# Reordering a pipelined turn and the closing sequence of a fused RWKV-6 and Mixture-of-Depths kernel

## The chip, the cores and the metric

The kernel runs on one core of a Trainium2 chip. The metric is device time in microseconds of one execution. A core has a matrix engine (TensorE, PE in the profile), a vector engine (VectorE, DVE), an activation engine (ScalarE, ACT), a general one (GpSimd, POOL) and a queue for transfers (SyncE, SP). Each engine works through its own list of instructions in order and waits for the others through semaphores. PEld is TensorE's loading of weights.

## The reference

Two blocks follow one another. The first is a recurrent attention (RWKV-6): for each of 4 batches and 8 heads, over 768 steps with head size 48,

```python
cur = einsum('bhd,bhe->bhde', u[None] * kt, vt)
y[:, :, t] = einsum('bhd,bhde->bhe', rt, state + cur)
state = wt[:, :, :, None] * state + einsum('bhd,bhe->bhde', kt, vt)
```

Its output, heads side by side, is x of 4 x 768 x 384. The second (Mixture of Depths) takes in each batch the 128 rows with the highest score and adds a gated MLP to them alone:

```python
scores = einsum('bsd,d->bs', x, w_gate)
top_idx = argpartition(-scores[b], capacity)[:capacity]
ye = maximum(xe @ w1, 0) @ w2          # 384 -> 1024 -> 384
out[b, top_idx] = x[b, top_idx] + sigmoid(scores[b, top_idx])[:, None] * ye
```

## The kernel before

The time axis is cut in chunks of 128 steps, six to a batch, 24 in all. Within a chunk the recurrence becomes matrix products: `scans` multiplies up the decays from both ends (two VectorE scans, from right and from left, read from the transposed w in PSUM), `scaled` makes K and R from the transposed k and r, `scores` multiplies them (ps_s), `masked` keeps the strictly earlier steps (sc), `outputs_t` multiplies sc with v and R with the state carried over (ps_yt), and `carry_products` and `carry` make the next state (kv, then mid and state). `back` transposes K back into kt, which only `carry_products` reads. The diagonal term, r times k times u summed over a head, is made apart: `own_products` (two GpSimd products), `own_values` (eight ScalarE sums, each an activation and a read of the accumulator, lines L293, and then a GpSimd product with v, L297). `rows_out` transposes the result to rows (ps_y), copies it out on ScalarE, adds the diagonal term on GpSimd and stores it. `row_products` and `row_sums` make the row's score. `range_check` sums over w on ScalarE (junk), for a check at the end.

The order is written by hand: `turn(i)` issues the steps of up to five neighbouring chunks, from chunk i + 2 (decays) to chunk i - 2 (comparing scores). Every engine takes its instructions in the order in which they are issued there. `loads(i + 5)` issues the inputs of the turns to come on SP's queue, in buffers that rotate over four or five chunks; in the first turns one weight tile is loaded per turn as well.

For the choice of rows, `compared_t` transposes a chunk's scores over all partitions (ps_e, in the bank of psK) and copies them to `every` on ScalarE; `compared` compares the chunk with earlier ones and with itself (`ahead`, with counts in `lost`). When a batch is complete, `mixture(b)` becomes a generator that goes on piece by piece: ranks by 21 small matmuls with ones (ps_r) and three small VectorE operations; `pick`, a comparison of the ranks with slot numbers; ps_i, the row numbers; an indirect gather of 128 rows (xe); their transposition; and last the gate (scr_x on GpSimd, a sum and an exponential on ScalarE, two small VectorE operations). Each yield carries a place, "half" or "end", and `mix(place=...)` goes on only where the place fits.

`forward` is the MLP of one batch, a generator too, of 8 pieces of ps_h (three 128x128 matmuls, each two instructions) and 8 of ps_f; then ye and an indirect scatter. `fed_in_turn` puts up to three pieces into a turn, except for batch B - 2, whose MLP is kept for the end, where it stands between the steps of the last batch. The last batch's ps_f is made in two halves of columns, each with its own ye and scatter.

Pools of PSUM with one buffer each: psW (w transposed), psS (scores and outputs), psY (rows), psK (kv, ps_e, ranks, row numbers), psM (MLP); psT (transposed k, r, K) has two. An instruction that takes a buffer waits until the one before it in that buffer has been read.

After the last turn the code lists the pieces by hand, then `checked()` reduces the range check and loads its result in a register of every engine (L264), which decides whether a general version has to run. For these inputs it doesn't.

## Time and profile before

| | us |
|---|---|
| median of 3 runs | 223.97 |
| lowest, highest | 223.69, 226.28 |
| the profiled execution, its own time | 226.24 |
| its span, first to last instruction | 224.4 |
| TensorE busy in the span | 197.57 (88%) |
| VectorE | 164.20 (73%) |
| ScalarE | 143.46 (64%) |
| GpSimd | 135.01 (60%) |

All rows of the profile come from one execution. Its own time is 1.84 us longer than the span from the first instruction to the last. A line such as L236 is the kernel's line, or that of a helper (L223 makes all transpositions, L281 makes K and R). The mean granted clock of TensorE over the span is 0.99. "idle" is the time in which an engine stood still before an instruction, and the arrow names what ended it. Durations of neighbouring instructions on an engine overlap a little, so the pitch from start to start is used where instructions are added up.

### The profile page before, as it was taken

What the parts mean: (1) busy time and instruction counts of PE and PEld (TensorE: products, weight loads), DVE (VectorE), ACT (ScalarE), POOL (GpSimd) and SP (SyncE); (2) the same over time, 40 slices, a digit from 0 to 9 for tenths busy, and PEclk for the clock granted to TensorE, in tenths of its full rate; (3) what the DMA queues carried; (4) which work ended last, traced back from release to release, by engine and by line L of the source; (5) the groups of instructions that cost most, each with busy time, mean ns of one, the idle gap of its engine ahead of it and who ended that gap; (6) DMA issues with size and microseconds to landing.
All of it is one profiled execution on the core that took longest, in us unless ns stands there. A gap on an engine that the chain in (4) does not pass through costs nothing.

```text
span 224.4 us, 6400 instructions
## 1 busy us (share of the span) xinstructions
PE 197.6 (88%) x2306; PEld 162.9 (73%) x2306; DVE 164.2 (73%) x370; ACT 143.5 (64%) x697; POOL 135.0 (60%) x158
## 2 busy tenths in 40 slices
PE   2699998898798699998999999989999989896990
PEld 1489877776676578977877788879787768764990
DVE  6979978899897977779987798698869863632010
ACT  6256977987777577777867686895766784512110
POOL 2335988776785498477558579864854965413011
PEclk9999999999999999999999999999999999998898
DMA  7999999998999788775996597479611201102000
GB/s 122 183 166 178 187 180 233 189 215 222 222 220 186 167 202 173 108 144 99 137 151 129 86 174 158 114 141 162 133 46 36 73 35 38 72 0 75 1 22 25
DMA packets 105687, 29.20 MB, mean 130 GB/s; under 512 B 100512, under 2 KB 104896, under 8 KB 105648
## 3 DMA queue, kind: packets, MB, share of 16 engines
q1 hardware_dynamic: 105104, 27.14, 67.3%
q0 software_dynamic: 544, 1.57, 2.3%
q8 instruction: 20, 0.33, 0.6%
q14 instruction: 19, 0.16, 0.2%
HBM read 23.20 MB, written 5.51 MB: 128 GB/s over the span
## 4 chain that ended last, share of the span: by engine, by line
PE 39%; ACT 28%; DVE 21%; issue 8%; POOL 1%; DMA 1%; POOLq 0%; DVEq 0%
ACT rk L293 13%; PE ps_t L223 8%; DVE right_buf L236 7%; PE ps_s L306 6%; PE ps_f L570 6%; PE ps_h L547 5%; ACT junk L270 4%; PE ps_yt L335 4%; DVE left L248 3%; ACT x L365 3%; PE ps_kv L396 3%; ACT kt L320 3%; DVE ahead L449 3%; PE ps_w L223 3%; PE ps_y L223 2%
## 5 line engine op out<-in xcount | busy, mean ns | idle before, releaser
L293 ACT ACTIVATE rk<-rk 128x48 f32<-128x48 f32 x192 | 43.8, 240 | 0.0
L367 POOL TENSOR_TENSOR x<-x,vo 128x384 f32<-128x384 f32 x23 | 23.0, 1001 | 30.4 <-ACT x L365 27.7
L293 ACT ACTIVATION_READ_ACCUMULATOR rk<-rk 128x1 f32 x192 | 38.0, 198 | 0.0
L315 DVE TENSOR_TENSOR sc<-ps_s,before_f 128x512 f32<-128x512 f32 x48 | 30.8, 682 | 4.1 <-PE ps_s L306 3.1
L248 DVE TENSOR_TENSOR_SCAN left<-ps_w,from_left 128x511 f32<-128x511 f32 x24 | 30.7, 1280 | 0.9
L236 DVE TENSOR_TENSOR_SCAN right_buf<-ps_w,from_right 128x511 f32<-128x511 f32 x24 | 29.2, 1218 | 0.7 <-PE ps_w L223 0.5
L306 PE MATMUL ps_s<-R,K 48*128 48x128 f32 x384 | 28.8, 291 | 0.1
L335 PE MATMUL ps_yt<-sc,v_buf 128*64 128x128 f32 x384 | 27.1, 284 | 1.6 <-PE ps_w L223 1.2
L547 PE MATMUL ps_h<-xeT,w 128*128 128x128 f32 x192 | 26.9, 293 | 1.8 <-DVE x L361 0.7
L286 POOL TENSOR_TENSOR rk<-r_buf,k_buf 128x384 f32<-128x384 f32 x24 | 24.1, 1006 | 7.2 <-DMA r_buf<-in_r_dram 7.2
L306 PEld LDWEIGHTS ps_s<-R,K 48*128 48x128 f32 x384 | 24.1, 193 | 4.3 <-issue 3.7
L547 PEld LDWEIGHTS ps_h<-xeT,w 128*128 128x128 f32 x192 | 24.4, 203 | 3.3 <-ACT xeT L514 1.2
L335 PEld LDWEIGHTS ps_yt<-sc,v_buf 128*64 128x64 f32 x384 | 21.4, 140 | 6.1 <-issue 2.8
L287 POOL TENSOR_TENSOR rk<-rk,u_bc 128x384 f32<-128x384 f32 x24 | 24.1, 1004 | 2.5 <-DMA u_bc<-in_u_dram 0.7
L372 POOL TENSOR_TENSOR scr<-x,wg_bc 128x384 f32<-128x384 f32 x23 | 23.0, 1000 | 1.8
L570 PE MATMUL ps_f<-w,hid 128*128 128x384 f32 (+1 forms) x80 | 23.8, 432 | 0.0
L320 ACT COPY kt<-ps_t 128x512 f32<-128x512 f32 x24 | 13.8, 575 | 14.4 <-PE ps_t L223 14.4
L281 DVE TENSOR_TENSOR R<-ps_t,left 128x512 f32<-128x512 f32 x24 | 16.5, 688 | 8.8 <-ACT x L365 2.7
L297 POOL TENSOR_TENSOR vo<-v_buf,own 128x384 f32<-128x384 f32 x24 | 19.9, 830 | 3.4 <-ACT rk L293 3.4
L223 PE MATMUL ps_w<-ident,w_buf 128*128 128x128 f32 x96 | 15.8, 291 | 4.8 <-DVE from_right L208 4.1
L348 ACT COPY yt<-ps_yt 128x512 f32<-128x512 f32 x24 | 14.1, 587 | 9.2 <-PE ps_yt L343 7.7
L449 DVE SCALAR_TENSOR_TENSOR ahead<-ps_e,score,after_f 128x128 bf16<-128x128 f32 x24 | 8.4, 350 | 15.7 <-ACT every L436 15.7
(98 smaller groups left out, 377.2 us busy)
## 6 DMA issues: line engine op xcount, KB each, us to landing
w_buf<-in_w_dram SPq DMA_DIRECT2D x24, 192.0 KB, 4.6
k_buf<-in_k_dram SPq DMA_DIRECT2D x24, 192.0 KB, 4.7
r_buf<-in_r_dram SPq DMA_DIRECT2D x24, 192.0 KB, 5.2
v_buf<-in_v_dram SPq DMA_DIRECT2D x24, 192.0 KB, 4.2
out_dram<-x SPq DMA_DIRECT2D x24, 192.0 KB, 2.5
w<-in_moe_w_dram SPq DMA_DIRECT2D x3, 512.0 KB, 5.9
w<-in_moe_w_dram SPq DMA_DIRECT2D x4, 384.0 KB, 6.2
u_bc<-in_u_dram SPq DMA_DIRECT2D x1, 192.0 KB, 4.6
```

The source lines that it names most:

```text
L223: nc.tensor.transpose(ps[:, j, :], src(j), ident)
L236: nc.vector.tensor_tensor_scan(out=flat[:, W - 2::-1], data0=wt[:, W - 1:0:-1], data1=from_right.rearrange("p j t -> p (j t)")[:, W - 2::- ...
L248: nc.vector.tensor_tensor_scan(out=left.rearrange("p j t -> p (j t)")[:, 1:W], data0=wt[:, 0:W - 1], data1=start.rearrange("p j t -> p (j ...
L286: nc.gpsimd.tensor_mul(rk, r_bufs[n % NBUF][:, :, 0:D], k_bufs[n % NBUF][:, :, 0:D])
L287: nc.gpsimd.tensor_mul(rk, rk, u_bc)
L293: nc.scalar.activation(out=rk[:, h, :], in_=rk[:, h, :], func=AF.Copy, accum_out=o[:, h:h + 1])
L306: nc.tensor.matmul(ps[:, q, j, :], t["K"][rows, j, :], t["R"][rows, j, :], start=True, stop=True,)
L315: nc.vector.tensor_mul(t["sc"][:, q], ps[:, q], _heads(before_f, HP))
L335: nc.tensor.matmul(ps[half(c), j % 2, j // 2, :], vt[:, 2 * j + q, :], t["sc"][:, q, j, :], start=(j < 2), stop=(old is None), skip_group_ ...
L367: nc.gpsimd.tensor_add(x, x, vo.rearrange("p h d -> p (h d)"))
L547: nc.tensor.matmul(ps[:, q, :], w1[:, dc, (f0 + q) * L:(f0 + q + 1) * L], xeT[:, dc, :], start=(dc == 0), stop=(dc == NDC - 1),)
L570: nc.tensor.matmul(ps, hid[:, fc, :], w2[:, fc, cols], start=(fc == 0), stop=(fc == NFC - 1))
```

## The change

The steps of a turn are issued in another order, some are split, and the closing sequence is another. What each engine's list shows:

- In the turn: `own_values` (ScalarE) right after `scores`; the second GpSimd product of `own_products` becomes `own_weights`, later in the turn; the product with v becomes `own_results`, later too; the one-element copy of `scans` becomes `first_left`, after `back`; `range_check` goes ahead of the outputs and `row_sums` ahead of the scans.
- `compared_t` and `compared` become one step, ahead of `masked`. Its ps_e lies in psW instead of psK, and the copy to `every` comes after the comparisons.
- `back` is left out for the last chunk of a batch.
- `mixture`: the rank matmuls use minus one, run with the later chunk outermost, and one more matmul (identity times `lost`) adds the counts; one reduction makes the rank. Ranks and `pick` are made in one piece. `pick` is six operations of 128 columns with a bf16 source.
- `fed_in_turn` gives batch B - 2 at most one piece per call, where it gave none.
- The last batch's ps_f, ye and scatter are no longer halved.
- The last two chunks' rows are added and scored on VectorE, where it was the last one's alone.
- In the end all 16 pieces of the last batch's MLP are issued ahead of `checked()`, and the gate after it, since the transposition of xe is now reached before. On TensorE the matmul of the range check stands behind the last ps_f; on GpSimd and ScalarE the load of the register stands ahead of scr_x and its sum.
- Memsets that are left to the framework's choice of engine fall out in another way at the start; from_right goes from ScalarE to VectorE.

```diff
-    ones = consts.tile([L, L], BF16)
-    nc.vector.memset(ones, 1.0)
+    minus = consts.tile([L, 1], BF16)
+    nc.vector.memset(minus, -1.0)
...
-    slots = consts.tile([L, L], FP32)
+    slots = consts.tile([L, L], BF16)
...
-        nc.scalar.copy(out=left[:, 0, 0:1], in_=start[:, 0, 0:1])
...
+    def first_left(t):
+        start = from_left[t["n"] % len(from_left)]
+        nc.scalar.copy(out=t["left"][:, 0, 0:1], in_=start[:, 0, 0:1])
...
-        nc.gpsimd.tensor_mul(rk, rk, u_bc)
+
+    def own_weights(t):
+        nc.gpsimd.tensor_mul(t["rk"], t["rk"], u_bc)
...
+    def own_results(t):
         t["vo"] = lev.tile([L, H, D], FP32, tag="vo", name="vo", bufs=3)
         nc.gpsimd.tensor_mul(
-            t["vo"], v_bufs[t["n"] % VBUF][:, :, 0:D], o.to_broadcast([L, H, D])
+            t["vo"], v_bufs[t["n"] % VBUF][:, :, 0:D], t.pop("own").to_broadcast([L, H, D])
         )
...
     def back(t):
+        if chunks[t["n"]][1] == NCH - 1:
+            return
...
-        t["e"] = ps = psK.tile([L, L], FP32, tag="kv", name="ps_e")
-        nc.tensor.transpose(ps, score[:, b, ci:ci + 1].to_broadcast([L, L]), ident)
-        if ci < NCH - 1:
-            nc.scalar.copy(out=against[b][0][:, ci * L:(ci + 1) * L], in_=ps)
...
+        ps = psW.tile([L, L], FP32, tag="w", name="ps_e")
+        nc.tensor.transpose(ps, own.to_broadcast([L, L]), ident)
         if ci > 0:
             nc.vector.tensor_scalar(
                 out=ahead[:, ci, 0:lo], in0=every[:, 0:lo], scalar1=own, scalar2=None,
                 op0=ALU.is_ge, op1=ALU.add, accum_out=lost[:, ci, 0:1],
             )
         nc.vector.scalar_tensor_tensor(
-            out=ahead[:, ci, lo:hi], in0=t.pop("e"), scalar=own, in1=after_f,
+            out=ahead[:, ci, lo:hi], in0=ps, scalar=own, in1=after_f,
             op0=ALU.is_ge, op1=ALU.mult, accum_out=lost[:, ci, 1:2],
         )
+        if ci < NCH - 1:
+            nc.scalar.copy(out=every[:, lo:hi], in_=ps)
...
+        for e in range(NCH):
+            for c in range(e + 1):
                 nc.tensor.matmul(
-                    ps[:, c:c + 1], ahead[:, e, c * L:(c + 1) * L], ones[:, 0:1],
-                    start=(e == c), stop=(e == NCH - 1),
-                )
+                    ps[:, c, 0:1], ahead[:, e, c * L:(c + 1) * L], minus,
+                    start=(e == 0), stop=False, skip_group_check=True,
+                )
+            if e == NCH - 2 and ended:
+                yield "half"
+        against.pop(b)
+        nc.tensor.matmul(
+            ps.rearrange("p c k -> p (c k)"), ident, lost.rearrange("p c k -> p (c k)"),
+            start=False, stop=True, skip_group_check=True,
+        )
         rank = mod.tile([L, NCH], FP32, name="rank", bufs=2)
-        nc.vector.tensor_add(rank, lost[:, :, 0], lost[:, :, 1])
-        nc.vector.tensor_add(rank, rank, behind_n)
-        nc.vector.tensor_sub(rank, rank, ps)
-        yield "end"
+        nc.vector.tensor_reduce(out=rank, in_=ps, axis=AX.X, op=ALU.add)
...
-            nc.vector.tensor_tensor(
-                out=pick, in0=_heads(slots, NCH), in1=at.to_broadcast([L, NCH, L]),
-                op=ALU.is_equal,
-            )
+            for c in range(NCH):
+                nc.vector.tensor_scalar(
+                    out=pick[:, c, :], in0=slots, scalar1=at[:, c:c + 1], scalar2=None,
+                    op0=ALU.is_equal,
+                )
...
-        if not (feed or picked) or (feed or picked)[0][0] != B - 2:
-            fed(n, on=False)
+        kept = (feed or picked) and (feed or picked)[0][0] == B - 2
+        fed(min(n, 1) if kept else n, on=False)
...
     def turn(i):
+        soon = i >= N - 1
         step(own_products, i + 1)
         step(scores, i)
+        step(own_values, i)
         step(scaled, i + 1, "K", "right")
         step(carry, i - 1, work.get(i))
+        step(own_weights, i + 1)
+        if i < N:
+            step(compared, i - 2)
         step(masked, i)
         step(back, i)
+        step(first_left, i + 1)
         mix(place="half")
-        if i == N:
-            fed(2)
-        step(rows_out, i - 1, i == N)
-        if i == N:
-            row_scores_soon(work[N - 1], work[N - 1]["x"])
-        else:
-            step(row_products, i - 1)
-        step(own_values, i)
+        step(rows_out, i - 1, soon)
+        step(row_scores_soon if soon else row_products, i - 1)
+        step(own_results, i)
         fed_in_turn(PIECES // 2)
         step(inputs_t, i + 1, "R", r_bufs)
-        step(compared_t, i - 2)
         step(scaled, i + 1, "R", "left")
         step(decays_t, i + 2)
-        step(compared, i - 2)
+        step(range_check, i + 2)
         step(outputs_t, i)
+        if i == N - 1:
+            step(compared, i - 1)
         step(carry_products, i)
         fed_in_turn(PIECES - PIECES // 2)
         step(inputs_t, i + 2, "K", k_bufs)
+        if not soon:
+            step(row_sums, i - 1)
         step(scans, i + 2)
-        step(range_check, i + 2)
-        if i < N:
-            step(row_sums, i - 1)
...
         ended.append(True)
-        fed(2)
-        step(compared_t, N - 1)
+        mix(1000)
+        mixing.append([mixture(B - 1), "half"])
+        mix()
         step(compared, N - 1)
-        mixing.append([mixture(B - 1), "half"])
         fed(2)
         mix()
         fed(1)
         mix()
-        fed(3)
+        fed(NFC - 1)
         mix()
+        fed(1)
         fed(2 * NFC)
         outside = checked()
         mix(1000)
```

## The prediction

> **What bounds the kernel now.** I read the page's busy shares first (TensorE 197.57 us of a span of 224.4, then VectorE 164, ScalarE 143, GpSimd 135), then the chain of waits, then the table of waits, then busy time turn by turn, and last the timeline of the end. No engine fills the span, so the chain says what holds it. One turn of the steady stretch:

> ```profile
> 41.82 1.80 ACT rk L293 x16
> 44.16 1.15 DVE right_buf L236
> 45.93 0.62 ACT junk L270 x2
> 46.57 0.64 ACT junk L270 x2
> 47.78 0.47 ACT kt L320
> 48.25 0.44 ACT x L365 x2
> 48.69 1.80 ACT rk L293 x16
> ```

> The columns are start, length and work. From one rk to the next is 6.87 us, and the chain goes from ScalarE to VectorE and back: VectorE can't start its scans before ScalarE has done rk and `every`, and ScalarE stands at the one-element copy L247 until VectorE's reciprocal. The table of waits (total, times, longest) has both crossings:

> ```profile
> ACT left L247 <- DVE from_left L244: 22.7, 21, 2.6
> ...
> DVE ahead L449 <- ACT every L436: 15.7, 18, 2.5
> ```

> Neither engine is full: the two wait for each other. TensorE by turn (from one chunk's first ps_s to the next; columns are window, length, then busy time and count of PE, weight loads, DVE, ACT, POOL, then clock, DMA share, GB/s):

> ```profile
> 38.53:45.40 6.87, 6.25 (x86) 5.03 (x86) 6.14 (x14) 5.46 (x28) 5.25 (x7) 1.00 1.10 208
> ...
> 65.82:73.65 7.83, 6.87 (x108) 5.50 (x107) 6.23 (x16) 5.56 (x28) 5.47 (x7) 1.00 0.96 229
> 73.65:81.99 8.34, 6.50 (x92) 5.12 (x91) 7.10 (x16) 5.56 (x28) 5.12 (x7) 1.00 0.76 175
> ...
> 114.48:122.93 8.45, 8.45 (x114) 6.68 (x113) 6.49 (x17) 5.77 (x29) 5.47 (x7) 1.00 0.74 124
> ```

> Turns without MLP pieces leave TensorE idle 0.6 to 1.8 us; with three pieces (some 2.1 us) it is full. So the first third has room to lose, the rest little. Last, the end:

> ```profile
> 204.31 0.14 DVE L261 TENSOR_SCALAR wide<-ps_w 1x1 int32<-1x1 f32 x1 [0.28 <-PE ps_w L259]
> ...
> 205.25 1.00 POOL L522 TENSOR_TENSOR scr_x<-xe,wg_bc 128x384 f32<-128x384 f32 x1
> ...
> 207.36 0.16 DVE L531 RECIPROCAL gate<-gate 128x1 f32<-128x1 f32 x1
> ...
> 218.62 0.42 DVE L577 SCALAR_TENSOR_TENSOR ye<-ps_f,gate,xe 128x192 f32<-128x192 f32 x1 [2.12 <-PE ps_f L570]
> 219.87 0.99 POOL L580 DMA_INDIRECT out_dram<-ye,to  x1 [2.13 <-DMA out_dram<-ye,to]
> ```

> The range check (`wide`) and the gate's scr_x are done under the last MLP, long before ye needs the gate.

> **The loop, turns 2 to 22.** own_values goes ahead of the turn's other ScalarE work, L247 moves behind kt, `every` behind `ahead`, the compare ahead of `sc`. The mutual wait goes. What then sets a turn? By the pitches in the timeline, VectorE needs K 0.58, mid 0.26, own compare 0.27, sc 1.19, R 0.60, right 1.26, all 0.19, reciprocal 0.22, left 1.20 = 5.77, and for the compare with earlier chunks 0 to 0.80 by its place in the batch (mean 0.45): 6.2. TensorE: ps_s 1.09, K back 0.60, ps_y 0.49, r 0.49, ps_e 0.12, ps_w 0.58, ps_yt 1.02 + 0.62, kv 0.60, k 0.59 = 6.2. ScalarE: 1.80 + 0.25 + 0.47 + 0.09 + 0.44 + 1.33 + 0.50 + 0.51 = 5.4. GpSimd 5.3. So 6.87 becomes about 6.3, with TensorE and VectorE both nearly full.

> The change adds one wait here: ps_e now takes the single psW bank, so it waits for the left scan, and ps_w behind it waits until `ahead` and `every` have read ps_e. On TensorE, K back, ps_y, r and ps_w queue behind ps_e, and the right scan waits for ps_w. Walking it from ps_e at 0: `ahead` starts 0.35 to 0.8, `every` ends some 0.65 later, at 1.0 to 1.45; TensorE, busy with K, y and r, comes to ps_w at 1.7. Hidden by 0.25 or more; uncovered, the whole handshake would be 1.5 us a turn. L247, late behind kt, ends at 1.6 to 2.0 and R wants it at 1.8: nothing to 0.2.

> Skipping `back` for the last chunk of a batch takes 4 transposes (0.60) from TensorE and one kt (0.47) from ScalarE, four times. Its turn then has 5.0 us of TensorE work and VectorE decides, at 5.5 to 6.3.

> The mixture: two small adds of VectorE (0.2 each) become one reduce (bounds 0.16 and 0.3, from the small reduce of 0.19 at L257), two more copies a batch 0.2, and a matmul with 18 columns (0.1 to 0.3). The pick becomes six 128-column operations with a bf16 source. The trace has none; nearest is L445 at 128x128 (pitch 0.27, with an accumulator read of 0.08 in it): 0.2 each, 1.2 against 0.85; lower bound 0.08 each, as of tiny operations. Ranks and pick move a turn up, so ps_i no longer stands behind a fresh pick: it idled 1.64 in turn 9.

> [...] The old pick (0.93 to 0.96 us, two SBUF sources) never met a GpSimd operation in this trace: GpSimd was idle from 75.06 while it ran at 75.18, and likewise later. The new one falls beside x<-x,vo (1.0 us). [...]

> Turn sums: 2 to 4, 20.15 -> 18.85 (6.25 + 6.3 + 6.3). Turns 5 to 9, 36.59 -> 32.5 (5.7, 6.2, 7.1, 7.0, 6.5: VectorE in 5 and 6, then TensorE waiting once for sc). Turns 10 to 22 lose their TensorE idle of 4.0 us and two `back` (1.2) and get back some 1.0 for extra instructions and one VectorE-bound turn: -4.2. Together -9.6. I take off 1.9, some 0.09 a turn, for hand-overs that an addition of pitches doesn't see: -7.7.

> **The tail.** Before, from the last chunk's ps_s (186.59) to the gather's issue (201.11) is 14.52. After: ps_s 1.09; ps_e and `ahead` to 1.75; sc to 2.94; ps_yt to 4.62; yt and one MLP piece to 5.5; ps_y 6.05; x and score on VectorE to 7.25; two pieces and 15 rank matmuls keep TensorE until 8.05; ps_e, own compare to 8.7; but two pieces stand in front of the last six ranks, to 9.7; lost, reduce 10.35; picks 11.5, ps_i chasing them; gather at about 12.0. Gain 2.5. It lands 3.2 later at 15.2, but seven ps_f pieces (4.7) hold TensorE to 16.2; ps_x then, against 18.45: -2.2.

> Those seven pieces fill the gap in which TensorE went cold:

> ```profile
> 206.13:209.50 3.37, 3.37 (x16) 3.37 (x17) 0.37 (x3) 0.82 (x3) 0.12 (x1) 0.51 0.08 27
> 209.50:213.00 3.50, 3.50 (x33) 3.50 (x33) 0.00 (x0) 0.60 (x1) 0.00 (x0) 0.99 0.00 0
> ```

> Granted clock 0.51, 16 matmuls where 33 fit next. [...] After the change only 0.6 us (xeT) stays idle; ps_h takes 48 x 0.128 = 6.1, not 7.06. [...] ps_f's end comes 3.2 earlier counted from ps_s.

> Then the loss. The new order issues all 16 pieces of the last batch before the range check, and the gate's part after it. The range check's matmul now stands behind the last ps_f, the register load of `wide` (0.515 on GpSimd, 0.464 on ScalarE) behind that, and GpSimd's scr_x and ScalarE's sum behind the load, with ye and the scatter waiting for the gate. From the end of ps_f: ps_w to `wide` and load 0.39 + 0.515, to scr_x 1.05; scr_x to reciprocal's end 2.27 (205.25 to 207.52); 0.62 for a whole ye (its 128x384 row); 0.28 to the scatter: 4.25. Before, the second scatter left 1.29 after ps_f's end, as it waited for the first one's landing. +3.0. One scatter of whole rows for two: its landing is 3.0 against 2.4, +0.3 taken. Tail: -3.2 + 3.0 + 0.3 = +0.1. TensorE's second MLP pieces moved into turn 23 are in this walk.

> Start: memsets change engines; from_right ends near 3.5 on VectorE while ps_w starts at 4.10: nothing, at most 0.4.

> **Sum.** 224.4 - 7.7 + 0.1 = 216.8 of span. The profiled execution took 226.24, 1.84 around the span, and lies at the top of the three runs (223.69, 223.97, 226.28); I take the same -7.6 from the median: 216.4.

> **Rivals.**
> - *The turns shrink, the tail pays* (0.15). The gather is not earlier or the clock still drops: the 3.2 is missing: 219.6. For: two MLP pieces stand ahead of the last ranks. Against: TensorE's work there is counted.
> - *DMA holds the first third* (0.12). The share is 1.10 at 208 GB/s in the turns that also load weights. Turns 2 to 9 keep their length, only 4.2 less 1.0 is won: 220.9. Against: past the start no wait there is for a load, which are issued turns ahead.
> - *The psW handshake* (0.08), on the other side. If ScalarE comes late to `every` (rk in front of it still running), ps_w and the right scan follow. The ScalarE round of x, GpSimd's two products, row sum, rk, `every` adds to 5.6; beyond 6.3 it decides, and at 7.2 the eight early turns gain 0.3 each and the full ones a bubble of as much on TensorE: 21 x 0.3 = 6.3 less 2.4 from `back` and 2.4 from the mixture's move (some 1.9 in turn 9, 0.5 in turn 8), and +0.1: 225.6.
> - *No hand-over losses* (0.10): -9.6, tail -0.5: 213.9.
> - Forecast, 216.4, own range 214.6 to 218.8 (0.55).

> **Numbers.** A measurement of this kernel tells some 2% from no change, so faster is below 219.5: forecast 0.55, no losses 0.10, about half of the tail case 0.07 and a little of DMA 0.02: 0.74. Slower than 228.4 needs the handshake at more than its price: 0.05. The rest 0.21. The range 213.7 to 221.2 leaves out the handshake and the outer edges.

> **What would show it.** Right: L247's successor no longer waits; turns 3 and 4 near 6.3; turn 9 near 6.5; the gather some 12 us after the last ps_s; clock near 1 through the last ps_h; and, on the bad side, over 4 us from the last ps_f to the only scatter. Wrong: waits of ps_w for `every`, or of the right scan for ps_w, in every turn; early turns still at 6.9; the pick stretched to a microsecond.

## The result, and the profile after

| | before | after |
|---|---|---|
| median, us (4 runs each) | 225.12 (223.69 to 226.62) | 215.79 (215.43 to 216.8) |
| ratio, 95% interval | | 0.9592 (0.9505 to 0.9679) |
| the profiled execution | 226.24 | 215.43 |
| its span | 224.4 | 213.6 |
| start, up to ps_s of chunk 2 | 25.25 | 24.27 |
| turns 2 to 22 | 161.34 | 151.70 |
| from the last chunk's ps_s to the end | 37.81 | 37.63 |

The forecast was 216.4. The three parts of the span changed by -0.98, -9.64 and -0.18, in all -10.8, where the forecast had 0, -7.7 and +0.1. The medians differ by 9.3, less than the spans, since the profiled execution lay near the top of its runs before and is the lowest one after. In the medians and ranges from here on all runs count, in the ratios only those within 1.5% of the fastest of the same kernel (with three moves six of ten, with the compare alone three of four).

The chain of waits (start, length, work), one turn of the same stretch that was shown of before:

```profile
36.28 1.09 PE ps_s L313 x16
...
38.94 0.45 PE ps_w L223 x4
39.39 0.19 issue
39.58 1.09 PE ps_yt L344 x16
...
42.45 1.09 PE ps_s L313 x16
```

Before, the chain went from ScalarE to VectorE and back. Here every piece is TensorE's own, and a turn takes 6.17 us where it took 6.87. Over the whole span 80% of the chain lies on TensorE, where it was 39%, with 28% on ScalarE and 21% on VectorE. The table of waits (total, times, longest):

```profile
ACT yt L357 <- PE ps_yt L352: 17.4, 19, 2.0
ACT every L460 <- DVE ahead L455: 12.9, 14, 1.4
...
ACT left L255 <- DVE from_left L244: 1.5, 1, 1.5
```

ScalarE's wait for the reciprocal has gone from 22.7 us to 1.5; VectorE's wait for `every` (15.7) is no longer there. ScalarE waits elsewhere instead, and in the turn shown those waits cost nothing: the chain doesn't pass through it. Busy time by turn (window, length, then busy time and count of PE, weight loads, DVE, ACT, POOL, clock, DMA share, GB/s):

```profile
36.21:42.38 6.17, 5.96 (x87) 5.05 (x86) 6.07 (x14) 5.50 (x30) 5.23 (x7) 1.00 1.01 229
...
68.09:75.30 7.21, 6.36 (x92) 5.17 (x91) 7.00 (x18) 5.02 (x27) 4.73 (x6) 1.00 1.05 201
106.98:115.64 8.66, 8.66 (x115) 6.89 (x115) 7.86 (x20) 5.60 (x30) 5.22 (x6) 1.00 0.72 129
```

In the first, TensorE and VectorE are both nearly full, as the walk through the turn had said. In the second, VectorE is at 7.00 of 7.21: there the pick of the turn before is paid (below). In the third, full of MLP, TensorE fills the turn. The closing sequence, from the timeline:

```profile
204.22 0.15 DVE L264 TENSOR_SCALAR wide<-ps_w 1x1 int32<-1x1 f32 x1 [11.07 <-PE ps_w L262]
205.10 0.99 POOL L536 TENSOR_TENSOR scr_x<-xe,wg_bc 128x384 f32<-128x384 f32 x1 [10.76 <-DVE wide L264]
...
207.39 0.62 DVE L578 SCALAR_TENSOR_TENSOR ye<-ps_f,gate,xe 128x384 f32<-128x384 f32 x1
208.29 1.02 POOL L581 DMA_INDIRECT out_dram<-ye,idx  x1 [2.20 <-DVE ye L578]
```

ps_f ended at 204.06. All four rows stand behind it: VectorE and GpSimd had waited 11 us for the range check's matmul, and the scatter leaves 4.23 after ps_f's end, where the second one of before left 1.29 after it. Busy time in a window over the last ps_h (columns as in the table by turn):

```profile
193.30:196.67 3.37, 3.37 (x30) 3.37 (x31) 0.00 (x0) 0.35 (x1) 1.03 (x1) 1.00 0.15 58
```

30 matmuls at a clock of 1.00, where 16 at 0.51 stood in an equal window before.

### The profile page after: what moved, and what is told of

Read it like the earlier page. It is cut to its first block, busy times and chain, and to the rows that moved or that the text cites. A ratio compares the mean times of both kernels' runs of the same rounds, so it can differ in the third digit from the quotient of the medians.

```text
span 213.6 us, 6385 instructions
## 1 busy us (share of the span) xinstructions
PE 190.9 (89%) x2282; PEld 157.4 (74%) x2282; DVE 166.3 (78%) x388; ACT 140.3 (66%) x688; POOL 131.5 (62%) x155
## 4 chain that ended last, share of the span: by engine, by line
PE 80%; ACT 4%; DVE 3%; issue 3%; DMA 3%; POOL 2%; SPq 2%; POOLq 0%
PE ps_t L223 13%; PE ps_s L313 11%; PE ps_yt L344 11%; PE ps_h L561 11%; PE ps_f L571 10%; PE ps_yt L352 5%; PE ps_kv L406 5%; PE ps_y L223 4%; PE ps_w L223 4%; PE ps_e L449 3%; DMA k_buf<-in_k_dram 3%; ACT rk L298 2%; SPq L132 1%; DVE sc L322 1%; PE ps_r L474 1%
## 5 line engine op out<-in xcount | busy, mean ns | idle before, releaser
L298 ACT ACTIVATION_READ_ACCUMULATOR rk<-rk 128x1 f32 x192 | 36.1, 188 | 0.0
L376 POOL TENSOR_TENSOR x<-x,vo 128x384 f32<-128x384 f32 x22 | 22.1, 1005 | 19.4 <-ACT x L374 19.2
L247 DVE TENSOR_TENSOR_SCAN left<-ps_w,from_left 128x511 f32<-128x511 f32 x24 | 30.7, 1281 | 0.9
L236 DVE TENSOR_TENSOR_SCAN right_buf<-ps_w,from_right 128x511 f32<-128x511 f32 x24 | 29.1, 1211 | 0.9 <-PE ps_w L223 0.8
L344 PE MATMUL ps_yt<-sc,v_buf 128*64 128x128 f32 x384 | 26.3, 278 | 2.4 <-PE ps_w L223 1.7
L561 PE MATMUL ps_h<-xeT,w 128*128 128x128 f32 x192 | 25.4, 280 | 1.1 <-ACT xeT L528 0.8
L344 PEld LDWEIGHTS ps_yt<-sc,v_buf 128*64 128x64 f32 x384 | 20.7, 136 | 6.8 <-PE ps_w L223 3.3
L561 PEld LDWEIGHTS ps_h<-xeT,w 128*128 128x128 f32 x192 | 22.9, 192 | 2.4 <-ACT xeT L528 1.3
L571 PE MATMUL ps_f<-w,hid 128*128 128x384 f32 x64 | 23.8, 499 | 0.3 <-ACT hid L566 0.3
L381 POOL TENSOR_TENSOR scr<-x,wg_bc 128x384 f32<-128x384 f32 x22 | 22.0, 1002 | 1.7
L284 DVE TENSOR_TENSOR K<-ps_t,right_buf 128x512 f32<-128x512 f32 x24 | 16.2, 677 | 6.2 <-PE ps_t L223 6.2
L422 POOL TENSOR_TENSOR state<-mid,all 128x192 f32<-128x192 f32 x16 | 8.1, 507 | 16.9 <-PE ps_s L313 11.5
```

What stands on the lines that cost most here:

```text
L236: nc.vector.tensor_tensor_scan(out=flat[:, W - 2::-1], data0=wt[:, W - 1:0:-1], data1=from_right.rearrange("p j t -> p (j t)")[:, W - 2::- ...
L247: nc.vector.tensor_tensor_scan(out=left.rearrange("p j t -> p (j t)")[:, 1:W], data0=wt[:, 0:W - 1], data1=start.rearrange("p j t -> p (j ...
L284: nc.vector.tensor_mul(out, t.pop(name + "t"), t.pop(by))
L298: nc.scalar.activation(out=rk[:, h, :], in_=rk[:, h, :], func=AF.Copy, accum_out=o[:, h:h + 1])
L344: nc.tensor.matmul(ps[half(c), j % 2, j // 2, :], vt[:, 2 * j + q, :], t["sc"][:, q, j, :], start=(j < 2), stop=(old is None), skip_group_ ...
L561: nc.tensor.matmul(ps[:, q, :], w1[:, dc, (f0 + q) * L:(f0 + q + 1) * L], xeT[:, dc, :], start=(dc == 0), stop=(dc == NDC - 1),)
```

## Experiments: which move makes the loop faster

Turn n is the time from chunk n's first ps_s to the next chunk's. The theory after the result was that of the prediction: the mutual wait of ScalarE and VectorE held the turn, and three moves end it. The rival was that one of them does all. First each move alone in the kernel before. Ratios in this part are to the kernel before.

**The copy of one element behind kt.**

```diff
-        nc.scalar.copy(out=left[:, 0, 0:1], in_=start[:, 0, 0:1])
...
         step(back, i)
+        step(first_left, i + 1)
```

> The kernel before with one edit: the one-element copy L247 leaves the scans and stands behind kt, as in the changed kernel. Ring theory (ScalarE waits for VectorE's reciprocal and VectorE for ScalarE's every; cutting one of the two crossings is enough): early turns fall from 6.87 to about 6.3, ScalarE's wait for the reciprocal (22.7 us) goes, time 3 to 4 us under the kernel before (225.1), near 221.5. Rival (each of the three moves gives its share of the loop's gain): about 1 us less, 224. Rival (the copy is tiny and its wait idle time that costs nothing): no difference.

Measured: 224.28, ratio 0.9946 (0.9917 to 0.9975). The wait at the copy is gone (1.4 us left of 22.7), early turns are 6.49 to 6.56, and VectorE still waits 13.7 us for `every`; turns 2 to 22 are 2.0 shorter. Cutting this crossing is not enough for the 221.5 of the ring theory: the gain is that of its first rival, and the other half of the mutual wait stays. How far such a sum repeats: the filler kernel (below) has the loop of the kernel before, and there turns 2 to 22 took 162.13 for 161.34, the 0.8 coming with a fall of TensorE's clock to 0.50 for 3.4 us in turn 9.

**The sums rk early.**

```diff
         step(scores, i)
+        step(own_values, i)
...
-        step(own_values, i)
+        step(own_results, i)
```

> The kernel before with one edit: the eight ScalarE sums rk are issued right behind ps_s, ahead of kt and x, the GpSimd product stays where it was. Ring theory: both crossings stay, the same work goes round in the same ring, early turns stay at 6.87 and the time at 225 within 1 us. Rival (the sums' place is what frees the loop): 3 us less, 222.

Measured: 223.14, ratio 0.9897 (0.985 to 0.9944). Turns 3 and 4 stay at 6.88, as the ring theory said, but the time falls by more than it allowed: turns 2 to 22 are 1.8 shorter, nearly all of it in turns 11 to 22 (-1.6), and the tail is 1.9 shorter. 1.6 of that is the last ps_h, whose clock did not fall in this execution (see the fillers below); up to its start the tail is 0.2 shorter.

**The compare in one step, ahead of sc, with ps_e in psW.**

The body of `compared` is the changed kernel's, with `every` after the comparisons.

```diff
+        step(compared, i - 2)
         step(masked, i)
...
-        step(compared_t, i - 2)
...
-        step(compared, i - 2)
```

> The kernel before with one edit: compared_t and compared become one step ahead of sc, ps_e lies in psW, every is copied after the comparison. Ring theory: VectorE no longer waits for ScalarE's every (15.7 us go), so the ring is cut at its other crossing: early turns about 6.3, 3 to 4 us less, near 221.5. Handshake rival (ps_e between two uses of the one psW buffer makes the right scan wait): early turns at 6.9 or more, 225 or slower.

Measured: 221.96, ratio 0.9866 (0.9803 to 0.9928): early turns 6.34 to 6.37, turns 2 to 22 shorter by 5.1, as the ring theory had it. (The trace is of the fastest of the four executions, 220.29.)

**All three.** If each took away a part of the mutual wait, they should add up.

> The kernel before with the three moves of the loop together (the copy behind kt, the sums early, the compare ahead of sc); back, mixture, MLP pieces and the end as before. In the changed kernel turns 2 to 22 took 9.6 us less than before; the compare alone took 5.1 off them, the copy 2.0, the sums 1.6. If they cut the same ring, the three together give little over the compare alone: 6, early turns 6.1, time near 220. If they add up: 8.7, time near 217.

Measured: 225.35 (223.2 to 228.23), ratio 0.9958 (0.9914 to 1.0001): nothing that can be told from no change. The mutual wait is gone (VectorE's wait for `every` is not in the table, ScalarE's at the copy is 1.4), but turns 3 and 4 take 6.78 and 6.77; turns 2 to 22 are 2.3 shorter, less than with the third move alone. The theory falls in this form. The chain of waits of this kernel shows what has taken the place of the old wait:

```profile
26.03 1.80 ACT rk L296 x16
27.84 0.16 ACT every L454
...
28.04 0.66 PE ps_w L223 x4
28.70 1.02 PE ps_yt L340 x16
...
30.37 0.59 ACT yt L353
30.96 0.62 ACT junk L273 x2
...
32.81 1.80 ACT rk L296 x16
```

This is a closed ring of 6.78 us (26.03 to 32.81). ps_w needs psW, which `every` has to read out first; `every` stands behind rk; rk stands behind yt, the range check (junk, two sums, 1.33) and the row's sum; yt waits for ps_yt, which stands behind ps_w. It is the handshake over psW, the slower rival of the prediction, in being, though by another way round than the prediction walked. In the changed kernel the range check stands ahead of yt. The new theory: that move, which is in the list of the change and which the prediction doesn't price, takes 1.33 us out of the ring and brings it to about 5.4, under the 6.2 of TensorE's and VectorE's own work. Two kernels test it, one from each side.

**The changed kernel with the range check put back.**

```diff
-        step(range_check, i + 2)
         step(outputs_t, i)
...
         step(scans, i + 2)
+        step(range_check, i + 2)
```

> The changed kernel with one step put back: the range check's two ScalarE sums (junk, 1.33 us) are issued behind the scans again, as before the change, so that on ScalarE they stand between yt and the row sum. The ring theory: through the single psW buffer the turn is a closed ring (every 0.25, ps_w 0.66, ps_yt 1.64, yt 0.58, then junk 1.33, row sum's scr 0.51, the sums rk 1.80, every again: 6.77 us), as found in the kernel before with the three moves of the loop. Turns 3 and 4 go from 5.9 to 6.0 back to 6.6 to 6.8, turns 2 to 9 lengthen by 3 to 5 us, and of the turns that TensorE fills (10 to 22) some by 0.2 to 0.4 each: 219.5 to 223 us, ACT waits at yt for ps_yt and PE at ps_e for ACT scr. Rival, that the place of the range check doesn't matter since ScalarE is not full (its sum is 5.4 us): 215.8, within 0.5%.

Measured: 225.17 (223.94 to 227.1), ratio 0.9968 (0.9924 to 1.0013). This one step undone takes back the whole gain, more than I had expected. Turns 2 to 22 take 161.64, against 161.34 before the change; turns 3 and 4 take 7.10 each. The ring is there, but not the one that I had drawn:

```profile
34.48 1.80 ACT rk L298 x16
36.29 0.15 ACT every L460
...
37.01 0.44 ACT x L374 x2
...
38.60 1.01 POOL scr L381
...
40.25 0.61 ACT junk L273 x2
...
41.59 0.85 ACT rk L298 x8
```

In the changed kernel's order the row's sum comes ahead of the scans, so a range check behind the scans stands after the sum and doesn't overlap with GpSimd: ScalarE's x, GpSimd's two products, the sum, junk, rk, `every`, kt, and x again, 7.11 us from rk to rk. Without junk that is 5.8, under the turn's 6.2. (2.0 of the loss lies in turn 10 alone, where TensorE stood 2.27 us at ps_h for xeT until 86.86 and the granted clock was 0.50 from 87 to 90; the other turns lose 8.0.)

**The three moves and the range check ahead of the outputs.** Kernel before, nothing else of the change.

```diff
+        step(range_check, i + 2)
         step(outputs_t, i)
...
         step(scans, i + 2)
-        step(range_check, i + 2)
```

> The kernel before with the three moves of the loop that together gained nothing (sums rk early, first_left behind kt, compare ahead of sc with ps_e in psW) and a fourth: the range check ahead of the outputs. Nothing else of the change (back, mixture, pick, tail are as before). The ring theory: the ring loses 1.33 us, to 5.4, under the 6.2 of VectorE's and TensorE's own work, so turns 3 and 4 come to 6.0 to 6.3, turns 2 to 22 gain 5 to 8 us of the kernel before instead of 2.3, and the time is 217.5 to 220.5. Rival, that the psW handshake itself eats the gain of the three moves whatever stands behind yt: 224 to 226, early turns 6.7 to 6.8.

Measured: 220.53 (219.86 and 221.2), ratio 0.975 (0.9672 to 0.9827). Turns 3 and 4 take 6.03 and 6.17, those of the changed kernel to 0.01 us (6.03, 6.17), and turns 2 to 22 take 153.27: -8.1 to before. In the early turns every piece of the chain is TensorE's again. With the three others in, the range check's place is worth 5.8 us of the loop (159.03 to 153.27); alone it wasn't tried. The total, of two runs only, shows less, as the tail is 3.6 longer than before. TensorE's clock fell to 0.50 for 3.4 us twice in it: after TensorE had stood at ps_e 1.89 us for the row's sum (turn 23 is still in the old order), and at the last ps_h, which took 7.25. (With three moves it stood there 1.88, the clock stayed at 1.00, the last ps_h took 5.62, and the tail was 38.1.) Turn 10 has such a fall too, at 78.92, and is 1.25 longer than after. What is left of the loop's gain in the changed kernel, 1.6, is `back` with 0.9 (below) and 0.7 that wasn't taken apart; the new order of the rank matmuls and of the MLP pieces was not tried alone.

| | turns 2 to 4 | 5 to 9 | 10 | 11 to 22 | 2 to 22 |
|---|---|---|---|---|---|
| before | 20.15 | 36.59 | 9.40 | 95.20 | 161.34 |
| three moves | 20.32 | 34.84 | 10.39 | 93.48 | 159.03 |
| and the range check | 18.12 | 32.70 | 11.61 | 90.84 | 153.27 |
| after | 18.11 | 32.92 | 10.36 | 90.31 | 151.70 |
| after, range check back | 21.74 | 35.00 | 12.34 | 92.56 | 161.64 |

## Experiments: the smaller parts

**`back` for the last chunks restored** in the changed kernel (its result is not used).

```diff
     def back(t):
-        if chunks[t["n"]][1] == NCH - 1:
-            return
```

> The changed kernel with back restored for the last chunk of every batch (work whose result isn't used). Theory of TensorE-bound turns: 0.6 us in the turns 11 and 17 and in the last, less in turn 5, which VectorE sets: 1.5 us slower, 217.3; at most 2.4. Rival (those turns are set by VectorE and ScalarE): less than 0.5 us.

Measured: 217.22, 1.43 above the changed kernel; ratio to before 0.9653 (0.9597 to 0.9709). The turns of the last chunks of full batches lengthen by 0.43 each (7.34 for 6.91, 6.67 for 6.24), the one in the first third by nothing (5.88 for 5.89), and the tail by 0.6. The price of the prediction, 0.60 in turns where TensorE is full and nothing elsewhere, holds but for 0.17.

**The old pick, one operation from two SBUF tiles, at the new place.**

```diff
-    slots = consts.tile([L, L], BF16)
+    slots = consts.tile([L, L], FP32)
...
-            for c in range(NCH):
-                nc.vector.tensor_scalar(
-                    out=pick[:, c, :], in0=slots, scalar1=at[:, c:c + 1], scalar2=None,
-                    op0=ALU.is_equal,
-                )
+            nc.vector.tensor_tensor(
+                out=pick, in0=_heads(slots, NCH), in1=at.to_broadcast([L, NCH, L]),
+                op=ALU.is_equal,
+            )
```

> The changed kernel with the old pick, one operation of 128x768 with two fp32 sources in SBUF, in the new place. The six new operations took 1.07 us beside an idle GpSimd and 1.82 us beside x<-x,vo, one of them 1.00. [...]

Measured: 215.22, ratio to before 0.9548 (0.949 to 0.9606), not told from the changed kernel by its total. By its turns it is: turn 9 is 6.35 where it was 7.21, the others are equal. The timelines of VectorE and of GpSimd in turn 8, first the changed kernel's:

```profile
64.55 1.82 DVE L496 TENSOR_SCALAR pick<-slots,rank 128x128 bf16<-128x128 bf16 x6
65.14 1.02 POOL L376 TENSOR_TENSOR x<-x,vo 128x384 f32<-128x384 f32 x1 [0.65 <-ACT x L374]
```

and with the old pick:

```profile
64.61 0.96 DVE L495 TENSOR_TENSOR pick<-slots,rank 128x768 bf16<-128x768 f32 x1
65.20 1.23 POOL L376 TENSOR_TENSOR x<-x,vo 128x384 f32<-128x384 f32 x1 [0.65 <-ACT x L374]
```

Of the six operations the one that starts 0.07 after a GpSimd operation (65.21 and 65.14) takes 1001 ns instead of 250, as long as that operation, which is not slowed (1.02). The single one keeps its 0.96, and here it is GpSimd, 0.59 behind it, that takes 1.23 instead of 1.00. (A wait until the pick's end would make GpSimd's operation 1.37.) With four moves the single pick starts just behind a GpSimd product:

```profile
116.39 1.00 POOL L290 TENSOR_TENSOR rk<-rk,u_bc 128x384 f32<-128x384 f32 x1
116.46 1.74 DVE L484 TENSOR_TENSOR pick<-slots,rank 128x768 bf16<-128x768 f32 x1
```

and takes 1.74 itself; in the kernels with the sums early, three moves and four moves there are seven picks of 1.66 to 1.77. (Where GpSimd led by 0.01 to 0.02 alone, with the compare moved, it was GpSimd that took longer, 1.80.) In the three pairs shown the one that started later, by 0.07 to 0.59, took longer; why, no run here shows. Going by these three, cutting the work into six gives GpSimd five more chances to be first.

**The gate ahead of the last MLP, the range check at the very end.**

```diff
         fed(1)
-        fed(2 * NFC)
-        outside = checked()
         mix(1000)
         fed(1000)
+        outside = checked()
```

> The changed kernel with the end reordered: the gate of the last batch is issued ahead of its MLP and the range check behind everything. Serial-gate theory: from the last ps_f to the scatter 0.9 us instead of 4.27, time 3.3 us under the changed kernel (215.8), near 212.5. Rival (the end is set by the landing of earlier stores or by the register load, which now stands behind the scatter): less than 1 us.

Measured: 214.64, ratio to before 0.9511 (0.947 to 0.9552). A miss of 2.1. The scatter did leave 0.93 after ps_f's end, as expected, but the execution went on for 7.2 us after that. `wide` was ready at 205.76 and the span ended at 212.7: 6.9 us follow the range check, and at the very end it sets the finish, the scatter doesn't. Most of the 6.9 is one instruction: behind the register load TensorE's branch takes 3.92, to 210.30, where those of the other engines take 0.05 to 0.07; the last semaphores take 2.35 more. TensorE's branch takes 3.3 to 3.9 in every kernel here, but elsewhere it is over before the last scatter lands, and the span ends 2.05 to 2.07 after that landing. Here the scatter landed at 209.99, 4.49 after its issue. Why this branch takes so long stays open.

**Range check and gate both ahead of the last MLP.**

```diff
         fed(1)
-        fed(2 * NFC)
         outside = checked()
         mix(1000)
```

> The changed kernel with the range check and then the gate of the last batch issued right behind the transposition of xe, ahead of the last MLP. In the run with the check at the very end the scatter came 0.93 after the last ps_f, but 7.2 us followed it, against 5.3 in the changed kernel. Theory (some 7 us of closing work follow the range check's result, whatever else is done, and want to be hidden as well as the gate): scatter 0.9 after the last ps_f and 5.3 after that, TensorE's MLP starts 0.5 later because of the register load; span near 211, time near 213. Rival (the end after the scatter stays at 7 us): no better than that run, 214.6.

Measured: 212.66 (212.27 to 213.06), ratio to before 0.9433 (0.9381 to 0.9485). The scatter leaves 0.93 after ps_f's end, 4.7 more end the span, and from the last ps_s to the end it is 34.57 where the changed kernel has 37.63. That is the +3.0 that the prediction put on the gate, but the match is made of three parts: the scatter leaves 3.30 earlier behind ps_f and lands in 2.62 instead of 3.23, while ps_h starts 0.88 later, as TensorE first loads the register.

**Fillers for the clock.** In the kernel before, eight unused matmuls are put in the gap ahead of the last ps_x.

```diff
         outside = checked()
+        warm = psY.tile([L, HP, L], FP32, tag="y", name="warm")
+        for q in range(8):
+            nc.tensor.matmul(warm[:, q % HP, :], ident, ident, start=True, stop=True)
         mix(1000)
```

> The kernel before with eight unused 128x128 fp32 matmuls of the identity between the range check and the transposition of the last batch's rows, where TensorE stood still and the granted clock of the last batch's first ps_h pieces was 0.51; results unused, nothing else is changed. Clock theory: the fillers keep TensorE busy in that gap, the clock stays near 1.0, the last batch's ps_h take 5.5 to 5.7 us in place of 7.06 and the time is 1.0 to 1.6 us shorter (about 224.3 beside 225.7). Rival, that the clock drops on any account there, or that ps_h is slow for another reason: ps_h about 7, time unchanged within 0.3, or up to 0.5 longer by the fillers.

Measured: 226.31, ratio 1.0025 (0.9986 to 1.0063). The timeline of TensorE:

```profile
207.97 5.62 PE L547 MATMUL ps_h<-xeT,w 128*128 128x128 f32 x48 [0.57 <-ACT xeT L514]
```

The 48 matmuls take 5.62 (their clock 1.00) instead of 7.25, their weight loads 5.43 instead of the 7.06 that the prediction used, as the clock theory had it. But that doesn't show that the fillers did it. The same gap, 2.86 us with 0.71 of work in it, stands ahead of the last ps_h in five more kernels without fillers, and in three of them the clock stayed at 1.00 too. What differs is where the gap lies. With four moves the clock falls to 0.50 at 78.92, 184.73 and 201.80; each of these three lows lasts 3.41 us, and the falls are 31 and 5 such lengths apart. In the kernel before it falls at 206.18, for 3.41 us, and at 223.24, 5 such lengths later. Counted in beats of that length from the falls, TensorE's busy time in the beat that holds most of the gap is:

| kernel | beat, us | TensorE busy | clock in the next beat |
|---|---|---|---|
| before | 202.76 to 206.18 | 1.26 | 0.50 |
| four moves | 198.39 to 201.80 | 1.30 | 0.50 |
| copy behind kt | 199.56 to 202.98 | 1.32 | 0.50 |
| compare | 199.90 to 203.31 | 2.08 | 1.00 |
| three moves | 200.41 to 203.82 | 2.13 | 1.00 |
| sums early | 199.45 to 202.86 | 2.19 | 1.00 |
| before, with fillers | 203.60 to 207.01 | 2.15 | 1.00 |

**Both improvements, the closing sequence and the old pick, in the changed kernel.**

> The changed kernel with the check's closing sequence and the gate ahead of the last batch's MLP (which gave 212.66 us) and the pick as one operation of 768 columns from two SBUF tiles (which took 0.86 us off one turn and gave 215.22 against 215.79). If the two gains add: 211.8 to 212.3 us. If the turn's gain is absorbed later (TensorE full in turns 10 to 22) and only the place of the gate counts: 212.6. In the tail the single pick (0.96) in place of six operations (1.07) changes nothing or 0.1.

Measured: 212.44 (211.76 to 214.24), ratio to before 0.9383 (0.9328 to 0.9437). That beats both kernels, and can't be told from the closing sequence alone (0.9433), as the intervals overlap. The profiled execution is the slowest of the five and shows why the pick paid nothing in it: turn 9 is 6.36, and turn 10 is 12.46 instead of 10.36.

```profile
79.29 0.88 PE L525 MATMUL ps_x<-ident,xe 128*128 128x128 f32 x3 [1.84 <-DMA xe<-out_dram,idx]
```

The gather was issued at 72.65 and landed 6.5 us later (5.2 with the old pick alone, 5.6 in the changed kernel). TensorE stood 1.84 us for it, and its clock fell to 0.50 for the 3.4 us that followed. Why it landed later than in those executions no run here shows.

## Why the prediction was right, and where it was not

*The hit* is in part luck. The forecast took 7.6 off a median of 223.97; a fourth run (226.62) made that median 225.12, and the fall from there is 9.3, by the spans 10.8. What failed was small enough to stay within the range.

*The hand-over deduction* was the term that failed most. The prediction summed the turns to -9.6 and took off 1.9, "some 0.09 a turn, for hand-overs that an addition of pitches doesn't see". The loop gave -9.64. Turns 2 to 4 took 18.11 (predicted 18.85), 5 to 9 32.92 (32.5), 10 to 22 gave -3.9 (-4.2): the stretches miss by -0.7, +0.4 and +0.3, and their sum hits. Once no ring is longer than TensorE's work, its list runs on with hardly a gap: the chain has 0.19 of idle time in the turn shown.

*The mechanism* was told too simply. "The mutual wait goes" is true of the waits, but three moves that make it go gave nothing together that the time tells. The fourth step, the place of the range check, was in the prediction's sum of ScalarE only as 1.33 of 5.4. A sum of an engine's work doesn't see order; what was needed is the length of each closed ring through it. The prediction did walk one such ring, in its slower rival: "x, GpSimd's two products, row sum, rk, `every` adds to 5.6; beyond 6.3 it decides, and at 7.2" 225.6. With the range check put back the ring is 7.11 and the time 225.17, with 161.64 of loop. So the rival was real, and it was kept away by a move that I had not put a number on. That its price is nearly right is luck: it made every turn 0.3 longer, but against before the turns 2 to 4 are 0.5 longer each, 5 to 9 1.6 shorter and 11 to 22 2.6 shorter in all, and turn 10, with its low clock, is 2.9 longer. That the ring without junk is under the turn was right in the prediction; that one line decides it was not seen.

*The pick*: the prediction priced it by the row of another operation (1.2 against 0.85 a batch), and beside GpSimd's operation it took 1.82 against 0.96, +0.86. It cost that in turn 9 (7.21, predicted 6.5) and nothing in the turns full of MLP. The forecast's value did not have it.

*`back`*: right, within 0.17 a turn.

*The tail*: gather at 12.32 (predicted 12.0), ps_x at 16.2 (16.2), the scatter 4.23 after ps_f's end (4.25). ps_h took 5.43 by its weight loads, the measure in which it had been 7.06 (6.1 predicted), so ps_f ended 3.9 earlier and not 3.2; the end after the one scatter came 5.3 later where it was 4.5 after the second one, +0.8 and not +0.3, and all of it is the landing (3.23 for 2.44). The two misses nearly cancel: -0.2 for +0.1. That the 7.06 was there to be won belongs to the execution profiled before: in three of six kernels with the same gap ps_h took 5.43 all the same.

*The start* was put at nothing and is 0.98 shorter by chunk 2's ps_s. It can't be credited to the change: the filler kernel is the kernel before up to its last microseconds, and has that ps_s at 24.47 where the kernel before has it at 25.25, and the changed kernel with the range check put back has it at 25.23. Over the kernels here chunk 1's ps_s came between 17.98 and 19.62. What sets it in an execution stays open.

*The other rivals*: the tail did not pay (the gather is earlier, the clock 1.00). DMA did not hold the first third (turns 5 to 9 are 3.7 shorter), though it shows in turn 10, which is 0.96 longer than before: TensorE waits 0.92 there for the gathered rows, which took 5.6 us to land at a DMA share of 1.24, where before they took 3.4 at 0.83.

## What to carry to other kernels

When a turn is reordered by hand, don't add up engines only: draw each closed ring (a buffer's reader, what stands ahead of it on its engine, what that waits for) and compare its length with the fullest engine, for the order as it will be. A move can be worth nothing alone and everything beside others, so take steps out of the finished version as well as putting them one by one into the old one. At the end of a kernel put whatever the last store or the closing sequence waits for ahead of the last long stretch of matmuls. And before a microsecond is credited to a move, look whether the clock fell in one trace and not in the other: one fall was worth 1.6 us here, as much as most moves.

## What the runs showed that I had not expected

- TensorE's last branch takes 3.3 to 3.9 us. Hidden behind a scatter's landing it costs nothing; with the range check last it makes up most of the 6.9 us from `wide` to the end.
- An idle stretch of TensorE doesn't always lower its clock. 1.84 us at a gather and 1.89 at ps_e were followed by a low of 0.50, in another kernel 1.88 at the same ps_e was not, nor 0.92 at a gather. By the beats of 3.41 us the two at ps_e differ too: TensorE was busy 1.52 us in the beat ahead of the low, and 1.68 in the least busy one where there was none. The length of a gap alone does not tell.
- The same gather of 128 rows, in the first third with its loads, landed 3.3 to 3.9 us after its issue where the DMA share was under 1 until then, and 4.4 to 6.5 where it was 1.08 to 1.33; the last one, with little other traffic, after 3.1 to 3.2.
